# The two last sums of an output block: from VectorE reading PSUM to GpSimd reading a copy in SBUF

## The chip, the cores and the metric

The kernel runs on one core of a Trainium2 chip. The metric is the device time of one launch in microseconds (us). Three runs of the kernel before gave 1357.14, 1357.23 and 1366.95 us, so the median is 1357.23 us.

## The reference, cut to what matters

```python
def _moe2_ref(x, w_in, w_out):
    h = x @ w_in                 # (4608, 512) @ (512, 2048)
    g = h * np.cos(h)
    return (g @ w_out)           # (4608, 2048) @ (2048, 512)

def reference(**kwargs):
    attn_out = _attn_ref(q, k, v, g_norm)      # linear attention, RMS norm
    x = attn_out.transpose(0, 2, 1, 3).reshape(4608, 512)
    x = _moe_ref(x=x, ...)                     # 8 experts, the best one for each token
    return _moe2_ref(x=x, w_in, w_out)
```

Everything is float32. The change touches only the last function, and of it only the sums that make finished rows of the output.

## The kernel before, in words

The kernel has three stages. Attention and routing come first, then the experts, and from about 640 us to the end the last one, `_moe2_ref`, which this text calls the last stage. Each float32 product is done as three passes of TensorE (PE) over a high and a low part of both operands, so every result that feeds a product is split: ScalarE (ACT) writes the high part (`copy`, L1165-1166) and VectorE (DVE) subtracts it to get the low part (`sub`, L1171-1172).

In the last stage the 4608 tokens are cut into 9 blocks of 512 (`b`) and the 2048 hidden units into 8 slices of 256 (`q_`). One `step(i)` (L1258) handles one slice of one block, and there are 72 slices (`NS`). Both matrix products of a slice are done in Winograd's form, with 7 products of half-size blocks in place of 8. A step interleaves three things, all written out by hand in program order, and each engine works through its own instructions in that order:

- `h(...)`, the first product for slice `i`, into the PSUM banks `ha` (`xa`) and `hb` (`xb`), which DVE and ACT combine into the tiles `h` (`h1`, `h0`);
- for slice `i - 1` the rest of the cosine and the sums and splits that its second product needs;
- `o(...)`, the second product for slice `j = i - 2`, which adds into six PSUM banks, one for each of `a11`, `s2`, `a12`, `s3`, `a22` and `s1`. There is one bank of each name. In every step the `s1` product is the last one (L496).

The banks collect over the 8 slices of a block. With the block's last slice (`q_ == 7`, the flag `done`) and in the step after it (`q_ == 0` of the next block, the flag `after`) they are summed into output rows. `acc` holds a running sum of a seventh product, and two scratch tiles in SBUF, `E1` and `U2` (L1546), hold the partial sums: in the `done` step `E1` is the copy of `a11` (L1345), `U2 = E1 + s2` (L1356) and `acc = U2 + acc` (L1391); in the `after` step `E1 = U2 + s3` (L1318), the last reader of `U2`. What is left then is `late_sum` (L1218), called twice in the `after` step: it adds the bank `s1` to `E1` (call at L1358) and to `acc` (call at L1372), writes the right half of the 512 columns of the output tiles `o_sb1` and `o_sb0`, and issues for each tile two indirect DMAs (`out_row`, L1193) on GpSimd's (POOL's) queue, which put 128 rows each to their tokens' places. The profile calls `E1` "e", `U2` "u", the output tiles "o_sb" and the banks "o_s" and "o_a".

The first PE work of the next block that needs the bank `s1` is the `s1` product at the end of that same `after` step, so it waits until both sums have read the bank. There are 8 such boundaries between blocks. The end of the ninth block has its own function (`last_step`), with sums of its own.

Beside this, `pump()` (L1106) feeds in, step by step, the preparation of the next block's tokens (`tokens_of`, L368): DVE subtractions at L395 and L406, ACT copies at L401. Names for the lines that the prediction uses: `turns` (L1086, ACT), `parts` (L1089, DVE), `cosine` (L1092, ACT), the multiplications with the cosine at L1188 and L1325 (DVE), `add` (L1169, DVE). The weights stream in on SyncE's queue (`feed`, L513) and are not touched.

Of the kernel before, what the change touches and what calls it, by code (L numbers as in the profile page):

```python
# [14 lines left out]
ALU = mybir.AluOpType  # L15
# [21 lines left out]
def tile_kernel(ctx, tc, q, k, v, g_norm, emb, tau, w1, w2, w_in, w_out, out):  # L37
    nc = tc.nc
# [536 lines left out]
    if True:  # L575
        def pool(name, bufs, cx=actx, **kw):
            return cx.enter_context(tc.tile_pool(name=name, bufs=bufs, **kw))
# [60 lines left out]
        for i in range(2):  # L638
# [6 lines left out]
            out=ident, in_=ones, pattern=[[1, 128]], compare_op=ALU.is_equal, fill=0.0, base=0, channel_multiplier=-1  # L645
        )
        nc.gpsimd.affine_select(
            out=upper, in_=ones, pattern=[[1, 128]], compare_op=ALU.is_gt, fill=0.0, base=0, channel_multiplier=-1
# [11 lines left out]
        for i in range(2):  # L660
            nc.gpsimd.iota(
                out=nums[64 * i:64 * i + 64, :, 8], pattern=[[2 * S, 4]], base=i * S + 512, channel_multiplier=1
# [95 lines left out]
        def where(t):  # L758
            j, i = divmod(t, 9)
            return j, (2 * j + i // 4 if i < 8 else None), i % 4  # L760
# [224 lines left out]
        for t in range(NTILE):  # L985
            j, b, r = where(t)
# [60 lines left out]
    if True:  # L1047
# [55 lines left out]
        G, Y, bank = {}, {}, {}  # L1103
# [61 lines left out]
        def copy(out, in_):  # L1165
            nc.scalar.activation(out=out, in_=in_, func=ACTF.Copy)  # L1166

        def add(out, x, y):
            V.tensor_tensor(out=out, in0=x, in1=y, op=ALU.add)  # L1169

        def sub(out, x, y):  # L1171
            V.tensor_tensor(out=out, in0=x, in1=y, op=ALU.subtract)  # L1172

        def f32(x):
            return x.bitcast(F32)
# [17 lines left out]
        def out_row(b, t, th):  # L1193
            n = 4 * b + 2 * t + th
            ins = nc.gpsimd.indirect_dma_start(  # L1195
                out=out, out_offset=bass.IndirectOffsetOnAxis(ap=perm_i[:, n:n + 1], axis=0),
                in_=OUT[b][t][:, th], in_offset=None, bounds_check=NT - 1, oob_is_err=False,
            )
            tc.add_to_no_dep_group("rows", ins.ins)
            tc.declare_no_dep(ins.ins, group="rows", reason="every token has its own row")  # L1200

        def halves(x):
            return x.rearrange("p (t c) -> p t c", t=2)

        OUT = {}
# [3 lines left out]
        def bank_of(name, i):  # L1209
            if i == 0:  # L1210
                return any_bank("hps" if name == "ha" else "xp")[:, 0:256]
            elif (name, i) == ("ha", 2):
                p, name = ps_o, "o_s1"
            else:
                p = ps_h
            return p.tile([128, 512], F32, name=name, tag=name)[:, 0:256]

        def late_sum(b, t, x):  # L1218
            add(OUT[b][t][:, :, 256:512], halves(x), halves(bank[b, "s1"]))
            for th in range(2):  # L1220
                out_row(b, t, th)

# [35 lines left out]
        def step(i):  # L1258
# [4 lines left out]
            b, q_ = divmod(j, 8)  # L1263
            done = j >= 0 and q_ == 7
            after = j >= 8 and q_ == 0
# [11 lines left out]
            def o(kind="o"):  # L1277
                return out_product(pe(kind)) if j >= 0 else None
# [57 lines left out]
            if prev:  # L1336
                sub(s24[:, 1], r0[:, 1], s24[:, 0])
                copy(hi0, r0)
                copy(hi13, s13)
                copy(hi24, s24)  # L1340
                sub(lo0, r0, f32(hi0))
            if after:
                add(OUT[b - 1][1][:, :, 0:256], halves(E1), halves(bank[b - 1, "a22"]))
# [12 lines left out]
                add(U2, E1, bank[b, "s2"])  # L1356
            if after:
                late_sum(b - 1, 1, E1)  # L1358
            if new:
                xb = bank_of("hb", i)  # L1360
            h(xb, True)
# [6 lines left out]
            if done:  # L1368
                OUT[b] = [op.tile([128, 2, 512], F32, name=f"o_sb{t}", tag=f"o_sb{t}") for t in range(2)]
                add(OUT[b][0][:, :, 0:256], halves(E1), halves(bank[b, "a12"]))  # L1370
            if after:
                late_sum(b - 1, 0, Y["acc"])  # L1372
            if prev:
                sub(lo24, s24, f32(hi24))
            if new:
# [5 lines left out]
            if j >= 0 and q_ % 2:  # L1381
                t = o("t")
# [34 lines left out]
        for g in range(NC * 8 + LAG):  # L1417
# [21 lines left out]
            if g >= LAG:  # L1439
                c2, f2 = divmod(g - LAG, 8)  # L1440
                if g == 8 * NC - 1:
                    between = chain.from_iterable(layer2_parts(chunks[c2], x) for x in (5, 6, 7))
                    step(0)
                    store_y(chunks[c2])()
                elif g < 8 * NC:
                    layer2(chunks[c2], f2)
                if f2 == 7 and c2 < NC - 1:
                    flush = store_y(chunks[c2])
# [57 lines left out]
    if True:  # L1506
# [8 lines left out]
        op = pool("op", 1)  # L1515
# [30 lines left out]
        E1, U2 = (cc.tile([128, 512], F32, name=nm) for nm in ("e1", "u2"))  # L1546
        scr = lambda: sx.tile([128, 512], F32, name="sx", tag="sx")
        for i in range(1, NS + 2):
            b, q_ = divmod(i, 8)
            if i == (8 * b or 2) and b + 1 < NB:  # L1550
                coming[0] = tokens_of(b + 1, scr)
            step(i)
            for x in range(2 * i - 4, min(2 * i - 2, NB)):
                if x >= 0:
                    load_perm(x)
            if i == 8:
                permf.append(scr()[0:NTILE, 0:128])
                V.tensor_copy(out=permf[0], in_=perm_r)
            if i == 9:
                turn_perm()  # L1560
# [3 lines left out]
    if True:  # L1564
# [15 lines left out]
        with tc.For_i(0, n_more, 1):  # L1580
# [12 lines left out]
                out=osel, in0=osel, in1=oh.rearrange("p (o x) -> p o x", o=1).to_broadcast([128, 3, E]), op=ALU.mult  # L1593
# [54 lines left out]
            for m in range(NM):  # L1648
# [17 lines left out]
                for t, (i, n) in enumerate(TS):  # L1666
                    for x, (a, b_) in enumerate(PASS):
                        nc.tensor.matmul(
                            out=oc[t][0:n], lhsT=(hi, lo)[a][:, i:i + n], rhs=w[:, b_, 512:1024],
                            start=(m == 0 and x == 0), stop=(m == NM - 1 and x == 2),  # L1670
                        )
            for t, (i, n) in enumerate(TS):
# [3 lines left out]
                    out=out, out_offset=bass.IndirectOffsetOnAxis(ap=rows2[0:n, t:t + 1], axis=0),  # L1676
# [31 lines left out]
```

## Time and profile before

| | us |
|---|---|
| median of three runs | 1357.23 |
| the profiled execution's own time | 1357.04 |
| its span (first to last instruction) | 1355.5 |
| PE busy in the span | 1302.9 (96%) |
| DVE busy | 1102.2 (81%) |
| ACT busy | 846.2 (62%) |
| POOL busy | 175.4 (13%) |
| mean granted TensorE clock | 0.995 |

A row of a list of instructions in time order has the start in us, the duration in us, the engine, the line of the kernel, the operation, the tile written and the tiles read, and the count of instructions merged in the row; square brackets at the end hold the idle time of that engine just before, and what ended it. PE is the matmul, PEld the loading of its weights, which runs a little ahead of it. "POOL DMA_INDIRECT" is the time POOL takes to issue such a DMA. Consecutive DVE or ACT instructions overlap by some 0.1 us in these records.

### The profile page before, as it was taken

The numbers are of one execution on the slowest core, as the hardware profiler recorded it, in microseconds if no ns is written. First come the engines' busy times: TensorE is split into PE (matmuls) and PEld (weight loads), VectorE is DVE, ScalarE is ACT, GpSimd is POOL, SyncE is SP. The second block draws the span as 40 slices with busy tenths as digits, with TensorE's granted clock in tenths as the row PEclk, the third lists the DMA queues.
The fourth block names the chain that finished last, engine by engine and source line by source line (L and its number), as shares of the span: only waits on it lengthen the run. The fifth ranks groups of instructions, "written<-read, shape, count | busy, mean of one in ns | idle before, by whom it ended". The sixth has DMA issues, their size and how long they took to land.

```text
span 1355.5 us, 30321 instructions
## 1 busy us (share of the span) xinstructions
PE 1302.9 (96%) x10825; PEld 1279.5 (94%) x10825; DVE 1102.2 (81%) x2511; ACT 846.2 (62%) x1698; POOL 175.4 (13%) x286
## 2 busy tenths in 40 slices
PE   7998799999999999998999999999999999999997
PEld 6886799999999999998999999999999999999997
DVE  2567867788989888866889898888989889798876
ACT  4667454677666776545666666676666766666663
POOL 1234132113220000000001010000101001010101
PEclk9999999999999999999999999999999999999998
DMA  9999485788888798659998888888889889888884
GB/s 276 290 326 284 133 246 129 209 249 261 251 249 272 253 281 274 211 163 329 339 320 296 284 293 269 290 285 299 284 267 309 271 290 294 284 291 271 262 284 136
DMA packets 238102, 359.31 MB, mean 265 GB/s; under 512 B 26045, under 2 KB 114913, under 8 KB 236729
## 3 DMA queue, kind: packets, MB, share of 16 engines
q1 hardware_dynamic: 221480, 297.20, 69.3%
q0 software_dynamic: 16448, 60.08, 14.0%
q8 instruction: 89, 1.46, 0.4%
q14 instruction: 69, 0.56, 0.1%
q10 hardware_dynamic: 16, 0.02, 0.0%
HBM read 299.32 MB, written 57.89 MB: 264 GB/s over the span
## 4 chain that ended last, share of the span: by engine, by line
PE 66%; DVE 11%; issue 9%; DMA 5%; ACT 4%; SPq 3%; POOL 1%; POOLq 0%; ACTq 0%; DVEq 0%
PE ha L1124 12%; PE y L274 10%; PE hb L1124 9%; PE o_s L1137 9%; PE o_a L1137 9%; PE hps L253 7%; PE hb L1137 3%; PE xp L253 3%; DMA vr<-in_v 1%; DMA wa<-ws 1%; SPq L599 1%; DVE gx L180 1%; DVE ring L141 1%; DVE o_sb L1169 1%; ACT gx L174 1%
## 5 line engine op out<-in xcount | busy, mean ns | idle before, releaser
L274 PE MATMUL y<-h,ring 128*128 128x304 f32 x1536 | 235.8, 302 | 1.3 <-DVE yo L284 1.3
L274 PEld LDWEIGHTS y<-h,ring 128*128 128x128 f32 x1536 | 220.1, 188 | 1.7 <-ACT h L259 1.5
L253 PE MATMUL hps<-xT,ring 128*128 128x304 f32 x1152 | 182.8, 308 | 2.7 <-DVE xT L233 1.8
L253 PEld LDWEIGHTS hps<-xT,ring 128*128 128x128 f32 x1152 | 165.0, 190 | 4.1 <-DVE xT L233 2.2
L1092 ACT ACTIVATE u<-u,half_pi 128x512 f32<-128x512 f32 x142 | 102.3, 720 | 56.8 <-DVE u L1089 56.8
L1195 POOL DMA_INDIRECT out<-o_sb,perm_i x36 | 48.6, 1350 | 684.8 <-DVE o_sb L1169 576.5
L1086 ACT ACTIVATE u<-h 128x512 int32<-128x512 f32 x142 | 89.7, 632 | 71.0 <-DVE h L1169 65.0
L1089 DVE SCALAR_TENSOR_TENSOR u<-h,u 128x512 f32<-128x512 f32 x142 | 97.9, 689 | 24.8 <-ACT u L1086 22.9
L1137 PE MATMUL o_a<-ring,hi 128*128 128x256 f32 x568 | 107.9, 282 | 0.0
L141 DVE TENSOR_TENSOR ring<-raw,ring 128x1024 fp32r<-128x1024 f32 x72 | 87.8, 1219 | 21.3 <-ACT ring L140 20.6
L1166 ACT ACTIVATE hi<-u 128x512 fp32r<-128x512 f32 x142 | 88.6, 624 | 26.5 <-DVE u L1172 26.5
L1172 DVE TENSOR_TENSOR lo<-u,hi 128x512 fp32r<-128x512 f32 x142 | 96.9, 683 | 0.0
L259 ACT ACTIVATE h<-hps 128x304 fp32r<-128x304 f32 x96 | 40.3, 419 | 78.6 <-PE hps L253 74.5
L1137 PEld LDWEIGHTS o_a<-ring,hi 128*128 128x128 f32 x568 | 87.2, 189 | 0.0
L1166 ACT ACTIVATE hi<-h 128x256 fp32r<-128x256 f32 (+1 forms) x142 | 74.2, 522 | 19.6 <-PE o_a L1137 9.1
L1325 DVE TENSOR_TENSOR h<-h,u 128x512 f32<-128x512 f32 x71 | 49.0, 690 | 44.5 <-ACT u L1092 44.1
L1137 PE MATMUL o_a<-ring,lo 128*128 128x256 f32 x284 | 79.7, 281 | 0.0
L1172 DVE TENSOR_TENSOR lo<-h,hi 128x256 fp32r<-128x256 f32 (+1 forms) x142 | 78.2, 550 | 0.0
L140 ACT ACTIVATE ring<-raw 128x1024 fp32r<-128x1024 f32 x72 | 75.8, 1053 | 0.0
L1137 PE MATMUL o_s<-ring,hi 128*128 128x256 f32 x376 | 71.9, 283 | 0.0
L253 PE MATMUL xp<-xT,ring 128*128 128x304 f32 x384 | 60.1, 303 | 2.4 <-DVE xT L233 2.4
L260 DVE SCALAR_TENSOR_TENSOR h<-hps,h 128x304 fp32r<-128x304 f32 x96 | 44.4, 463 | 18.2 <-ACT h L259 16.3
(333 smaller groups left out, 3374.2 us busy)
## 6 DMA issues: line engine op xcount, KB each, us to landing
wb<-ws SPq DMA_DIRECT2D x224, 256.0 KB
wa<-ws SPq DMA_DIRECT2D x167, 256.0 KB
raw<-in_moe_w SPq DMA_DIRECT2D x144, 256.0 KB
ring<-ws SPq DMA_DIRECT2D x113, 256.0 KB
wb<-wo SPq DMA_DIRECT2D x96, 256.0 KB
ring<-wo SPq DMA_DIRECT2D x75, 256.0 KB
wa<-wo SPq DMA_DIRECT2D x73, 256.0 KB
wo<-wa SPq DMA_DIRECT2D x52, 256.0 KB
```

What stands on the lines that cost most here:

```text
L140: nc.scalar.activation(out=w[:, 0], in_=raw, func=ACTF.Copy)
L141: nc.vector.tensor_tensor(out=w[:, 1], in0=raw, in1=w[:, 0].bitcast(F32), op=ALU.subtract)
L253: nc.tensor.matmul(out=p[:, 0:CH], lhsT=w[:, a, k * 128:(k + 1) * 128], rhs=c["xT"][b_][k], start=(n == 0), stop=(n == 11),)
L274: nc.tensor.matmul(out=c["y"][d][:, 0:CH], lhsT=w[:, a, 512 + d * 128:512 + (d + 1) * 128], rhs=h[b_], start=(f == 0 and i == 0), stop=(f ...
L1086: nc.scalar.activation(out=n, in_=p, func=ACTF.Copy, scale=TURN, bias=0.25)
L1089: V.scalar_tensor_tensor(out=u, in0=p, scalar=TURN, in1=n, op0=ALU.mult, op1=ALU.subtract)
L1092: nc.scalar.activation(out=u, in_=u, func=ACTF.Sin, scale=2 * math.pi, bias=half_pi)
L1124: nc.tensor.matmul(out=out, lhsT=w[:, a, k * 128:(k + 1) * 128], rhs=x[xi][:, b_, k * 256:(k + 1) * 256], start=(start and n == 0), stop=( ...
L1137: nc.tensor.matmul(out=o[:, th * 256:th * 256 + 256], lhsT=G[j, name][a][:, th * 128:th * 128 + 128], rhs=w[:, b_, 0:256], start=(start an ...
L1166: nc.scalar.activation(out=out, in_=in_, func=ACTF.Copy)
L1172: V.tensor_tensor(out=out, in0=x, in1=y, op=ALU.subtract)
L1325: V.tensor_tensor(out=r0, in0=r0, in1=two_of(Y["u", 0]), op=ALU.mult)
```

## The change

In the `after` step, ACT copies the bank `s1` into `U2` (free since L1318 has read it). The two sums of `late_sum` are made by POOL, from `E1` or `acc` and from `U2`, all in SBUF. The second call of `late_sum` moves up to stand right behind the first. The DMAs of `out_row` stay on POOL's queue, in the same order among themselves.

```diff
         def late_sum(b, t, x):
-            add(OUT[b][t][:, :, 256:512], halves(x), halves(bank[b, "s1"]))
+            nc.gpsimd.tensor_tensor(out=OUT[b][t][:, :, 256:512], in0=halves(x), in1=halves(U2), op=ALU.add)
             for th in range(2):
                 out_row(b, t, th)
...
                 copy(hi24, s24)
+                if after:
+                    copy(U2, bank[b - 1, "s1"])
                 sub(lo0, r0, f32(hi0))
...
             if after:
                 late_sum(b - 1, 1, E1)
+                late_sum(b - 1, 0, Y["acc"])
...
-            if after:
-                late_sum(b - 1, 0, Y["acc"])
             if prev:
                 sub(lo24, s24, f32(hi24))
```

## Rows read from the trace of the kernel before

**Rows 1.** The page's first part: busy time of each engine in the span.
```profile
PE 1302.9 (96%) x10825; PEld 1279.5 (94%) x10825; DVE 1102.2 (81%) x2511; ACT 846.2 (62%) x1698; POOL 175.4 (13%) x286
```
**Rows 2.** Waits of PE's matmuls, 640 to 1350 us: total, times, longest.
```profile
PE o_s L1137 <- DVE o_sb L1169: 4.0, 8, 0.5
```
**Rows 3.** The chain that ended last: the same group in every second step.
```profile
786.16 1.44 PE hb L1137 x12
...
807.10 1.43 PE hb L1137 x12
...
827.12 1.44 PE hb L1137 x12
```
**Rows 4.** PE and PEld in time order at one boundary.
```profile
796.74 0.40 PE L1137 MATMUL o_a<-wb,hi 128*128 128x256 f32 x2
...
798.10 0.47 PE L1137 MATMUL o_s<-wa,hi 128*128 128x256 f32 x2 [0.49 <-DVE o_sb L1169]
...
801.03 0.78 PEld L1124 LDWEIGHTS ha<-ring,wa 128*128 128x128 f32 x6
...
806.13 0.76 PEld L1124 LDWEIGHTS ha<-ring,wb 128*128 128x128 f32 x6
```
**Rows 5.** DVE in time order at the same boundary.
```profile
794.81 0.68 DVE L1172 TENSOR_TENSOR lo<-u,hi 128x512 fp32r<-128x512 f32 x1
...
795.41 0.41 DVE L1169 TENSOR_TENSOR h<-five,ha 128x256 f32<-128x256 f32 x1
...
795.74 0.68 DVE L1169 TENSOR_TENSOR o_sb<-e,o_s 128x512 f32<-128x512 f32 x1
...
796.67 0.68 DVE L1089 SCALAR_TENSOR_TENSOR u<-h,u 128x512 f32<-128x512 f32 x1
...
797.27 0.68 DVE L1169 TENSOR_TENSOR o_sb<-acc,o_s 128x512 f32<-128x512 f32 x1
...
799.31 0.69 DVE L1089 SCALAR_TENSOR_TENSOR u<-h,u 128x512 f32<-128x512 f32 x1 [0.16 <-ACT u L1086]
...
800.59 0.68 DVE L395 TENSOR_TENSOR sx<-xb,sx 128x512 f32<-128x512 f32 x1
...
805.66 0.41 DVE L1169 TENSOR_TENSOR h<-five,ha 128x256 f32<-128x256 f32 x1
...
806.83 0.69 DVE L1089 SCALAR_TENSOR_TENSOR u<-h,u 128x512 f32<-128x512 f32 x1 [0.43 <-ACT u L1086]
```
**Rows 6.** ACT in time order at the same boundary.
```profile
793.78 0.63 ACT L1166 ACTIVATE hi<-u 128x512 fp32r<-128x512 f32 x1 [0.37 <-DVE u L1172]
...
795.91 0.63 ACT L1086 ACTIVATE u<-h 128x512 int32<-128x512 f32 x1 [1.50 <-DVE h L1169]
...
800.62 0.36 ACT L1166 ACTIVATE one<-ha 128x256 f32<-128x256 f32 x1
```
**Rows 7.** ACT's copies of a whole bank, 740 to 1270 us: busy us, mean ns.
```profile
L1166 ACT ACTIVATE e<-o_a 128x512 f32<-128x512 f32 x7 | 4.1, 581 | 0.0
```
**Rows 8.** POOL in time order at the same boundary.
```profile
796.70 1.51 POOL L1195 DMA_INDIRECT out<-o_sb,perm_i  x1 [74.30 <-DVE o_sb L1169]
...
800.32 1.21 POOL L1195 DMA_INDIRECT out<-o_sb,perm_i  x1 [0.30 <-DVE u L1089]
```
**Rows 9.** POOL's groups by shape, whole span: busy us, mean ns, idle before.
```profile
L878 POOL TENSOR_TENSOR exc<-exc,ohc 128x8 f32<-128x8 f32 x16 | 3.3, 209 | 6.9 <-DVE ohc L873 6.3
...
L675 POOL MEMSET kvb<- 128x576 f32 x3 | 1.6, 572 | 0.0
L865 POOL TENSOR_TENSOR w<-w,tie 128x24 f32<-128x24 f32 x8 | 2.0, 254 | 32.7 <-DVE w L864 32.6
...
L643 POOL MEMSET ones<- 128x128 f32 x1 | 0.3, 271 | 0.0
```
**Rows 10.** DVE and POOL in time order near 117 us, in the first stage.
```profile
117.20 1.21 DVE L141 TENSOR_TENSOR ring<-raw,ring 128x1024 fp32r<-128x1024 f32 x1
...
117.28 1.20 POOL L879 TENSOR_TENSOR run<-exc,ohc 128x8 f32<-128x8 f32 x1
```

## The prediction, as put on record before the run

> **What bounds the kernel now.** I read the page's busy shares first, then the chain of waits that ended last, then PE's own waits in the last stage, and at last one boundary between two blocks on all engines in order of time. PE is busy 96% of the span [rows 1], so a change is worth what it takes off PE's waits, or what it adds to them. The chain runs through PE in almost every piece of the last stage. The reader is to look at one group that comes back in every second step: from 807.10 to 827.12 it takes 20.02 us, two steps with PE at its pace, and from 786.16 to 807.10 it takes 20.94 us [rows 3]. That longer pair holds a boundary, and the excess is 0.92 us. There are 8 boundaries [rows 2], so all that any change to the boundary can win is about 8 x 0.92 = 7.4 us, half a per cent.
>
> Where does the 0.92 us go? The list in time order shows three places. First, the six matmuls into `a22` begin at 796.74 and take 0.72 us as any six do (half of the 1.44 of twelve), so the `s1` product could start at 797.46; it starts at 798.10, released by the second late sum on DVE [rows 3, 4]. That is 0.64 us. Second, at 801.03 the weights of an `ha` product are loaded some 0.1 us late, behind ACT's copy `one`, which ends at 800.62 + 0.36 = 800.98 [rows 4, 6]. Third, at 806.13 the same happens behind DVE's sum `h<-five,ha`, which ends at 805.66 + 0.41 = 806.07 [rows 4, 5]. The last two matter more than their size: ACT and DVE are late there too, so a PE that arrives earlier merely waits longer. DVE has no idle time between 799.31 and the 0.43 us ahead of 806.83 [rows 5].
>
> **The change part by part.** *The copy on ACT.* It follows the copy `hi24`, which runs from 793.78 to 794.41; a copy of a whole bank takes 0.58 us, so `U2` is ready about 794.9 [rows 6, 7]. ACT's next instruction starts at 795.91 after 1.50 us of idling for a DVE sum, so the copy lies inside that idle time and costs nothing; if the cover were gone it would cost 0.58 us of ACT's time. The bank is then free 2.5 us before 797.46, and PE's wait of 0.64 us goes away in full.
>
> *The two sums leave DVE.* They sit at 795.74 and 797.27 [rows 5], and DVE starts a following instruction some 0.6 us after the one before, so 1.2 us of DVE's time is set free. But not all of it comes out as earlier work. The next long DVE instruction, `parts` at 796.67, needs ACT's `turns`, which runs from 795.91 to 796.54 [rows 5, 6] and starts behind `h<-five,ha`, which does not move. So `parts` can start at 796.57, 0.10 us earlier. The second sum stood between `parts` and the low part of `s24`; without it that low part ends about 0.7 us earlier, and ACT's next `turns`, which overwrites what it reads, follows. By then the cosine and its multiplication are the later chain, and I get `parts` of the next half at about 798.9 in place of 799.31. So DVE and ACT gain about 0.42 us of the 0.64 that PE gains, and at 801.03 and 806.13 PE waits for them. With nothing else, the boundary gains 0.42 us.
>
> *The two sums on POOL.* The trace shows no POOL addition of this size. From below: a fill grows from 271 ns at 128 columns to 572 ns at 576, 0.67 ns a column [rows 9]; an addition has two inputs, and two such passes over 512 columns plus 0.2 us are 0.9 us. From above: POOL's additions take 209 ns at 8 columns and 254 ns at 24 [rows 9], 2.8 ns a column, which at 512 gives 254 + 488 x 2.8 = 1.6 us. I take 1.3 us, between the two; the addition rows are the same operation but a long way off, so both ends stay in the range. That POOL itself is busy longer costs nothing: it idles 74 us before each boundary [rows 8], the output tiles are not reused for most of a block, and `acc` is not overwritten before the next step.
> [...]
>
> *What the POOL sums do to DVE.* This decides the sign. Near 117 us a POOL addition of 8 columns, which takes 0.21 us elsewhere, takes 1.20 us [rows 9, 10]. It starts 0.08 us after a DVE subtraction with both inputs in SBUF and ends 0.07 us after that one. So a POOL instruction that reads SBUF stands still while DVE reads two SBUF tensors, and it got its turn as soon as that one DVE instruction was over. I read this as something that one of the two engines holds at a time, and conclude that a POOL sum will hold up a DVE instruction with two SBUF inputs in the same way, for the sum's whole duration. The trace before cannot show that side, since POOL's additions there are tiny; so its price goes from nothing to the whole 1.6 us, and I take the whole of the 1.3 us.
> [...]
>
> Now the schedule. The first POOL sum is ready about 795.05. DVE is then in a low-part subtraction (both inputs in SBUF) until 794.81 + 0.68 = 795.49 [rows 5], so the sum runs from 795.49 to 796.79. DVE's next two sums read PSUM and go on; `parts`, both inputs in SBUF, waits from 796.57 to 796.79. That costs 0.22 us, and the gain of 0.42 shrinks to 0.20. POOL then issues the two DMAs of the first tile; first to third such DMA is 800.32 - 796.70 = 3.6 us before [rows 8], so with the first starting 0.3 us behind the sum the second sum is ready at about 800.7. DVE is there in its stretch without idle time, in the preparation of tokens, with two SBUF inputs each; the instruction of 800.59, now at 800.39, ends at 801.07. The second sum takes over for 1.3 us, and the next DVE instruction starts at 802.37 where it would have started at 800.99: 1.38 us lost. Net on DVE: 1.38 - 0.20 = 1.18 us later than before. `h<-five,ha` then ends at 807.25 in place of 806.07, and PE, which waits for it at 806.13, is 1.18 us later than before. The `ha` product's neighbour `hb` waits for the same DVE stretch a little earlier, for less. PE has no idle time later to win that back.
>
> Sum: 8 x 1.18 = 9.4 us. The profiled execution took 1357.04 us, which stands 0.2 us below the median; 1357.0 + 9.4 = 1366.4 us, 0.7% slower. With a POOL sum of 0.9 us the first sum costs nothing and the boundary loses 0.98 - 0.42 = 0.56 us, in all 4.5 us (1361.5). With 1.6 us it loses 1.68 - 0.42 + 0.52 = 1.78 us, in all 14.2 us (1371.2).
>
> **The rivals.** *POOL does not hold DVE up.* If only POOL waits, or if the two share at a finer grain than an instruction, the gain of 0.42 us a boundary is left: 8 x 0.42 = 3.4 us, 1353.6 us. For it: no DVE row shows a delay beside POOL. Against it: those POOL instructions are too short to show one, and the 1.20 us row shows a whole instruction's exclusion. If ACT and DVE should keep up with PE after all, the ceiling of 7.4 us gives 1349.6.
> *POOL's sum is far slower than its rows say.* If it takes 2.5 us, DVE loses 2.58 - 0.42 + (2.5 - 1.08) = 3.6 us at a boundary, in all 29 us, 1386 us. It decides above 1.5 us, where the slowdown passes 1%. For it: 2.8 ns a column is read off two tiny shapes. Against it: nothing in the rows is slower than that.
> *The hold-up falls where DVE has time.* If the second sum comes to lie behind 806, where DVE idles 0.43 us and more, gain and loss cancel: about 1357 us. Against it: POOL's queue puts it at 800.7, six us too early.
>
> **How the numbers follow.** The hold-up as worked out: 0.57. No hold-up: 0.31. Cancelling: 0.05. Much slower sums: 0.07. The likeliest case has its own range of 1361.5 to 1371.2; the range that takes in the case without hold-up goes from 1352 to 1371. About 1% (13.6 us) is what a measurement of this kernel can tell from no change. Faster by more than that is beyond the ceiling of 7.4 us: 0.01. Slower by more needs sums of nearly 1.6 us or the slow case: 0.12. The rest, 0.87, is within 1%.
>
> **What would show it right or wrong.** PE's wait for `o_sb` at the `s1` product must be gone, and the copy of the bank must start about 794.3 into ACT's idle time. Two POOL additions of about 1.3 us must stand at each boundary, the first running to about 796.8, the second about 801 to 802.4. DVE must show a gap or a stretched instruction with two SBUF inputs beside the second of about its length. PE must show 8 new waits of over 1 us for `h<-five,ha` or `h<-two,hb`, and a pair of steps with a boundary must last about 22.1 us in place of 20.94. If the DVE instructions beside POOL's sums keep their usual spacing, the hold-up is wrong and the pair lasts about 20.5 us.

## The result, and the profile after

The changed kernel took 1369.44 us (median of 13 runs), beside 1361.33 us for the kernel before (also 13 runs, the first three among them): a ratio of 1.0079, 95% interval 1.0062 to 1.0097, so it is 0.8% slower. The profiled execution took 1365.98 us, against 1357.04 before. The forecast was 9.4 us or 0.7% slower, by POOL's sums holding up DVE.

PE's new waits come first. These are the waits of PE's weight loads in the last stage of the kernel after (what waited, on what; us in total, times, longest; PEld is the loading of PE's weights):

```profile
PEld hb L1124 <- DVE h L1169: 10.6, 7, 1.5
PEld ha L1124 <- DVE h L1169: 3.1, 8, 0.4
PEld ha L1124 <- ACT h L1166: 2.0, 8, 0.3
```

The wait for `o_sb` of [rows 2] is gone, and a wait for DVE's sums `h` has come, 1.5 us long at 7 of the 8 boundaries. At the boundary that the rows of before show (all of this trace runs 0.73 us earlier there), this is POOL in time order:

```profile
794.26 1.66 POOL L1219 TENSOR_TENSOR o_sb<-e,u 128x512 f32<-128x512 f32 x1 [73.81 <-ACT u L1166]
796.19 1.22 POOL L1195 DMA_INDIRECT out<-o_sb,perm_i  x1 [0.28 <-POOL o_sb L1219]
797.72 1.16 POOL L1195 DMA_INDIRECT out<-o_sb,perm_i  x1 [0.30 <-issue]
798.90 1.30 POOL L1219 TENSOR_TENSOR o_sb<-acc,u 128x512 f32<-128x512 f32 x1
```

DVE in time order, to be held against [rows 5]:

```profile
794.07 0.68 DVE L1172 TENSOR_TENSOR lo<-u,hi 128x512 fp32r<-128x512 f32 x1
794.68 0.41 DVE L1169 TENSOR_TENSOR h<-five,ha 128x256 f32<-128x256 f32 x1
795.01 0.41 DVE L1169 TENSOR_TENSOR h<-one,hb 128x256 f32<-128x256 f32 x1
795.85 0.69 DVE L1089 SCALAR_TENSOR_TENSOR u<-h,u 128x512 f32<-128x512 f32 x1 [0.43 <-ACT u L1086]
...
798.27 2.49 DVE L1089 SCALAR_TENSOR_TENSOR u<-h,u 128x512 f32<-128x512 f32 x1 [0.24 <-ACT u L1086]
...
804.57 0.41 DVE L1169 TENSOR_TENSOR h<-two,hb 128x256 f32<-128x256 f32 x1
...
806.44 0.41 DVE L1169 TENSOR_TENSOR h<-five,ha 128x256 f32<-128x256 f32 x1
```

The row to look at is the one at 798.27: the same instruction on the same shapes, 2.49 us in place of 0.69, and it ends 0.56 us after the second POOL sum (798.90 + 1.30 = 800.20). Beside the first POOL sum nothing is stretched (0.41, 0.41 and 0.69 us). Everything behind on DVE is late, and PE, in time order, waits for it:

```profile
785.27 0.40 PE L1137 MATMUL hb<-ring,hi 128*128 128x256 f32 x2
...
805.04 0.97 PE L1124 MATMUL hb<-ring,ring 128*128 128x256 f32 x6 [1.30 <-DVE h L1169]
...
806.91 0.97 PE L1124 MATMUL ha<-ring,wb 128*128 128x256 f32 x6 [0.18 <-DVE h L1169]
807.73 0.40 PE L1137 MATMUL hb<-wa,hi 128*128 128x256 f32 x2
```

The first and the last of these rows begin the group of [rows 3]: 807.73 - 785.27 = 22.46 us for the pair of steps with a boundary, where it was 20.94. On the way PE waits 1.30 us at an `hb` product, for DVE's sum `h<-two,hb`, and then 0.18 us at the `ha` product, for `h<-five,ha`. ACT did what was foreseen: the copy of the bank at 793.59 lies in idle time, of which 1.01 us is still left behind it.

```profile
793.59 0.58 ACT L1166 ACTIVATE u<-o_s 128x512 f32<-128x512 f32 x1
795.18 0.64 ACT L1086 ACTIVATE u<-h 128x512 int32<-128x512 f32 x1 [1.01 <-DVE h L1169]
```

Over all 8 boundaries the pairs took 178.4 us in place of 168.0, which is 10.4 us: 1.2 to 1.5 us at each of the first seven, 0.1 at the last. The two profiled spans differ by 8.9 us only, and the rest lies in other places: this execution reached the last stage 2.0 us sooner, and lost 0.6 us once ahead of a boundary. So the length of a boundary pair is the sharper measure, and it is used beside the ratios from here on. It repeats within 0.03 us over most boundaries of a trace (22.44 to 22.47 us at six of the eight here), while the medians of the kernel before, taken beside the runs below, lie between 1358.63 and 1361.33 us.

### The profile page after: what moved, and what is told of

It reads as the page before. It is cut to its first block, busy times and chain, and to the rows that moved or that the text cites. A ratio compares the mean times of both kernels' runs of the same rounds, so it can differ in the third digit from the quotient of the medians.

```text
span 1364.4 us, 30365 instructions
## 1 busy us (share of the span) xinstructions
PE 1308.6 (96%) x10825; PEld 1282.8 (94%) x10825; DVE 1109.0 (81%) x2495; ACT 849.8 (62%) x1706; POOL 190.6 (14%) x302
## 5 line engine op out<-in xcount | busy, mean ns | idle before, releaser
L1089 DVE SCALAR_TENSOR_TENSOR u<-h,u 128x512 f32<-128x512 f32 x142 | 112.5, 792 | 29.1 <-ACT u L1086 26.8
L1219 POOL TENSOR_TENSOR o_sb<-e,u 128x512 f32<-128x512 f32 x8 | 13.3, 1658 | 613.8 <-ACT u L1166 613.8
L1124 PE MATMUL ha<-ring,wb 128*128 128x256 f32 x390 | 57.9, 284 | 1.7 <-DVE h L1169 1.1
```

Source lines behind the costliest of these rows:

```text
L1089: V.scalar_tensor_tensor(out=u, in0=p, scalar=TURN, in1=n, op0=ALU.mult, op1=ALU.subtract)
L1124: nc.tensor.matmul(out=out, lhsT=w[:, a, k * 128:(k + 1) * 128], rhs=x[xi][:, b_, k * 256:(k + 1) * 256], start=(start and n == 0), stop=( ...
```

## The experiments

The theory is that a POOL instruction that reads SBUF keeps DVE from starting or finishing one with two SBUF inputs. Its rivals: the cost is in the copy or in the new order; each POOL sum costs its own length wherever it lies; any POOL work does it. "Pair" is that of the boundary shown above.

| kernel | pair, us | sum of the 8 pairs | ratio to before (95%) |
|---|---|---|---|
| before | 20.94 | 168.0 | |
| after | 22.46 | 178.4 | 1.0079 (1.0062 to 1.0097) |
| `a_copy_dve` | 20.95 | 167.5 | 0.9995 (0.9983 to 1.0007) |
| `b_first_pool` | 20.88 | 166.9 | 0.9988 (0.9974 to 1.0001) |
| `c_second_pool` | 22.30 | 177.3 | 1.0073 (1.0047 to 1.0100) |
| `d_sums_first` | 21.38 | 170.4 | 1.0028 (1.0009 to 1.0048) |
| `e_fill` | 20.63 | 165.1 | no ratio (one run) |
| `f_one_input` | 21.48 | 171.0 | no ratio (one run) |
| `g_late` | 20.63 | 165.1 | 0.9978 (0.9965 to 0.9992) |
| `h_a22_later` | 20.18 | 161.7 | 0.9953 (0.9935 to 0.9972) |
| `i_no_pool` | 20.12 | 161.3 | 0.9961 (0.9947 to 0.9975) |
| `j_a22_alone` | 20.94 | 168.0 | 1.0005 (0.9990 to 1.0020) |

**Both sums back on DVE, the copy kept** (`a_copy_dve`; edits are against the kernel after):

```diff
-            nc.gpsimd.tensor_tensor(out=OUT[b][t][:, :, 256:512], ...)
+            V.tensor_tensor(out=OUT[b][t][:, :, 256:512], ...)
...
-                late_sum(b - 1, 0, Y["acc"])      # back in its old place, behind parts_of
```

> Theory (a POOL sum that reads SBUF holds up DVE instructions with two SBUF inputs): with both sums back on DVE, reading the copy U2, no DVE instruction is stretched. PE's 0.64 us wait at the s1 product is gone, but DVE carries as much as before, so PE waits for ACT's copy and DVE's sum instead: a pair of steps with a boundary takes 20.8 to 20.95 us (20.94 before, 22.46 after the change), ratio 0.999 to 1.000. Rival (the copy into U2 on ACT, or the lost slot on ACT, costs the time): the pair stays near 22.4 us, ratio 1.007.

Measured: 20.95 us, no change from before. The copy costs nothing, and it wins nothing by itself. These are the waits of PE's weight loads in this kernel:

```profile
PEld ha L1124 <- ACT one L1166: 2.8, 7, 0.4
PEld ha L1124 <- ACT h L1166: 2.7, 8, 0.4
```

The 0.64 us saved at the `s1` product is waited for a little later, for two copies by ACT.

**One sum on POOL** (`b_first_pool`: the first; `c_second_pool`: the second; the other one on DVE, reading `U2`; in `b_first_pool` the second call of `late_sum` is also back in its old place):

```diff
-            nc.gpsimd.tensor_tensor(...)
+            (nc.gpsimd if t else V).tensor_tensor(...)      # b; c has (V if t else nc.gpsimd)
```

> Only the first sum on POOL, the second on DVE from U2 in its old place. Theory: the first sum falls where DVE reads PSUM or waits for ACT, so it holds up nothing that counts; POOL's addition shows some 1.6 us, no DVE instruction is stretched by over 0.2 us, the pair takes 20.8 to 20.9 us, ratio 0.998 to 1.000. Rival (each POOL sum costs DVE its own length wherever it falls): the pair takes some 21.7 us, ratio 1.004.

> Only the second sum on POOL, the first on DVE from U2. Theory: this sum alone makes the loss; one DVE instruction is stretched by 1.2 to 1.9 us, the pair takes 22.0 to 22.6 us, ratio 1.006 to 1.010. Rival (each POOL sum costs the same): some 21.7 us, ratio 1.004.

Measured: 20.88 and 22.30 us. The two sums are the same instruction on the same shapes; the first is free, and the second alone makes 22.30 - 20.94 = 1.36 of the 1.52 us. That excludes a fixed price for a POOL sum. In `c_second_pool` another DVE instruction is hit, a sum of 256 columns that takes 0.41 us elsewhere. DVE and then POOL in time order:

```profile
804.38 1.94 DVE L1169 TENSOR_TENSOR u<-h 128x256 f32<-128x256 f32 x1
```

```profile
804.71 1.31 POOL L1219 TENSOR_TENSOR o_sb<-acc,u 128x512 f32<-128x512 f32 x1
```

It ends 0.30 us after the sum, as the one of 512 columns ended 0.56 us after: most of the instruction's usual 0.41 or 0.69 us is still to be done when the sum ends.

**Both sums first, then the four DMA issues** (`d_sums_first`):

```diff
             nc.gpsimd.tensor_tensor(out=OUT[b][t][:, :, 256:512], ...)
-            for th in range(2):
-                out_row(b, t, th)
...
                 late_sum(b - 1, 0, Y["acc"])
+                for t in (1, 0):
+                    for th in range(2):
+                        out_row(b - 1, t, th)
```

> Both sums on POOL, right behind each other, then the four DMA issues. Theory that the hold begins while POOL still issues the DMA ahead of the second sum (so that DVE loses 1.80 us to a sum of 1.30): with no DMA ahead of it DVE loses at most 1.3 us, its instruction (now the first parts of the step, near 795.9) shows at most 2.0 us in place of 2.49, and the pair takes 21.8 to 22.1 us, ratio 1.004 to 1.006. Rival (the hold is the second sum's own, and longer than its record): the stretch stays at 1.8 us and the pair near 22.4 us, ratio 1.007.

Measured: 21.38 us, less than either theory gave. POOL and then DVE in time order:

```profile
795.61 1.66 POOL L1219 TENSOR_TENSOR o_sb<-e,u 128x512 f32<-128x512 f32 x1 [72.03 <-ACT u L1166]
797.22 1.82 POOL L1219 TENSOR_TENSOR o_sb<-acc,u 128x512 f32<-128x512 f32 x1
```

```profile
797.20 0.69 DVE L1089 SCALAR_TENSOR_TENSOR u<-h,u 128x512 f32<-128x512 f32 x1 [0.43 <-ACT u L1086]
797.81 1.78 DVE L1172 TENSOR_TENSOR lo<-u,hi 128x512 fp32r<-128x512 f32 x1
```

Here one can see both directions in four rows. DVE's `parts` came 0.02 us ahead of the second sum and ran its usual 0.69; the sum waited for it and took 1.82 us. DVE's next instruction then waited for the sum: 1.78 - 0.69 = 1.09 us lost, where it was 2.49 - 0.69 = 1.80 with two DMA issues ahead of the sum. The pair grows by less, 21.38 - 20.63 (`e_fill`, below, where nothing holds DVE) = 0.75 us, because DVE has idle time right behind: the 0.19 us that it idles ahead of L1188 in the kernel after are gone, and 0.16 of the 0.24 us ahead of the next `parts` are left. The sum also lies beside other instructions than before, so this run does not separate the DMA issue from the place.

**What of a POOL instruction holds DVE** (`e_fill`, `f_one_input`; the second sum alone is replaced, so the bank `s1` is missing from that quarter of the output, and in `e_fill` `acc` too):

```diff
+            if t:
                 nc.gpsimd.tensor_tensor(...)
+            else:
+                for _ in range(2):                                     # e_fill
+                    nc.gpsimd.memset(OUT[b][t][:, :, 256:512], 0.0)
...
+                nc.gpsimd.tensor_copy(out=OUT[b][t][:, :, 256:512], in_=halves(x))   # f_one_input
```

> As after the change, but in place of the second sum POOL only fills the same half of the tile, twice (the second sum is left out; POOL is busy about as long, some 1.1 us, and reads no SBUF tensor). Theory (POOL's reading of SBUF is what holds DVE): the instruction parts behind it takes its usual 0.69 us and the pair with a boundary takes 20.5 to 20.8 us in place of 22.46. Rival (any POOL instruction of that length holds DVE, or it is POOL's writing): parts is stretched by 1 us or more and the pair stays at 22 us or above.

> As after the change, but the second sum is a POOL copy of acc, one input in place of two (the bank's part of these columns is left out). Theory: one SBUF input is enough to hold DVE, for the copy's own length of 0.5 to 0.9 us and what it begins under the DMA issue ahead of it (0.5 us in the kernel after the change); parts takes 1.5 to 2.1 us, the pair 21.4 to 22.0 us. [...]

Measured: 20.63 and 21.48 us. POOL, then DVE, in `e_fill`:

```profile
800.83 1.16 POOL L1195 DMA_INDIRECT out<-o_sb,perm_i  x1 [0.30 <-issue]
801.99 1.13 POOL L1223 MEMSET o_sb<- 128x512 f32 x2
```

```profile
801.38 0.69 DVE L1089 SCALAR_TENSOR_TENSOR u<-h,u 128x512 f32<-128x512 f32 x1 [0.24 <-ACT u L1086]
801.99 0.42 DVE L1169 TENSOR_TENSOR u<-h 128x256 f32<-128x256 f32 x1
802.32 0.42 DVE L1172 TENSOR_TENSOR lo<-h,hi 128x256 fp32r<-128x256 f32 x1
```

And in `f_one_input`:

```profile
801.59 0.98 POOL L1222 COPY o_sb<-acc 128x512 f32<-128x512 f32 x1
```

```profile
800.97 1.12 DVE L1089 SCALAR_TENSOR_TENSOR u<-h,u 128x512 f32<-128x512 f32 x1 [0.24 <-ACT u L1086]
802.02 0.83 DVE L1169 TENSOR_TENSOR u<-h 128x256 f32<-128x256 f32 x1
```

1.1 us of POOL writing costs DVE nothing, and neither does the DMA issue ahead of it, in whose record `parts` starts: it takes its usual 0.69 us. A POOL copy with one SBUF input costs DVE 0.43 + 0.42 = 0.85 us, spread over two instructions, and the pair is longer by just that (21.48 - 20.63). So it is POOL's reading, and one input is enough. I had expected all of it in `parts` (1.5 to 2.1 us, measured 1.12), and a copy of 0.5 to 0.9 us, which was my estimate with no row behind it; the copy took 0.98.

**The second sum on DVE one step later** (`g_late`; the first stays on POOL):

```diff
             if new:
                 add(h0[:, 0:256], one, xb)
+            if j >= 8 and q_ == 1:
+                late_sum(b - 1, 0, Y["acc"])      # on DVE, from U2
+            if new:
                 parts_of(i, 1)
```

> First sum on POOL (which held up nothing), second on DVE from U2, one step later, ahead of parts, where DVE idles some 0.4 us. Theory: PE's wait at the s1 product is gone and DVE is free of both sums in its full stretch; left are PE's waits for the copy of h0 (0.3 us) and for the copy one (0.1 to 0.2 us): the pair takes 20.5 to 20.8 us, ratio 0.997 to 0.999. Rival (DVE's work at the boundary is conserved and PE waits for it anyway): 20.9 us, ratio 1.000.

Measured: 20.63 us, 0.9978. The early copy and a DVE free of both sums in its full stretch do win something: 0.31 us at a boundary. In the list of PE's waits one is left there, for ACT's copy into `h0` (8 times, up to 0.3 us).

**And DVE's sum with `a22` later** (`h_a22_later`, on top of `g_late`): the addition of L1343 goes behind `turns_of(i, 1)`, so that DVE makes the sum with `five`, for which `turns` waits, before it.

```diff
-            if after:
-                add(OUT[b - 1][1][:, :, 0:256], halves(E1), halves(bank[b - 1, "a22"]))
...
                 add(h1[:, 256:512], five, xa)
                 turns_of(i, 1)
+            if after:
+                add(OUT[b - 1][1][:, :, 0:256], halves(E1), halves(bank[b - 1, "a22"]))
```

> As the run before, and DVE's sum with the bank a22 moved behind the one with five, so that ACT's turns starts 0.6 us earlier. Theory (ACT's and DVE's chain through turns is what PE waits for after the s1 product): PE's waits for ACT's copies of h0 and ha shrink by most of their 0.45 us, the pair takes 20.1 to 20.5 us, ratio 0.995 to 0.998. Rival (these waits come from another place): no change from the run before.

Measured: 20.18 us where two undisturbed steps take 20.02, and a ratio of 0.9953: faster than both kernels. In this kernel POOL's sum starts 0.10 us after DVE's subtraction has ended (796.00 + 0.68 = 796.68) and takes 1.29 us, which is its own length. DVE's sum with `a22`, which has one input in PSUM, lies inside it and is not stretched:

```profile
796.78 1.29 POOL L1219 TENSOR_TENSOR o_sb<-e,u 128x512 f32<-128x512 f32 x1 [65.61 <-ACT u L1166]
```

```profile
796.93 0.68 DVE L1169 TENSOR_TENSOR o_sb<-e,o_a 128x512 f32<-128x512 f32 x1
```

**Which part of that wins** (`i_no_pool`: as `h_a22_later`, but both sums on DVE one step later; `j_a22_alone`: the kernel before with the `a22` sum moved and nothing else):

```diff
+            if j >= 8 and q_ == 1:                     # i_no_pool
+                late_sum(b - 1, 1, E1)                 # both on DVE
+                late_sum(b - 1, 0, Y["acc"])
```

> As the fastest run so far (a22 later), but without any POOL sum: both sums on DVE from U2, one step later. Theory (the gain comes from the order on DVE and the early copy of the bank, POOL's share is one sum of 0.6 us of DVE time): DVE has 0.43 us of idle time ahead of parts there for 1.2 us of sums, so parts comes some 0.8 us late in that step and PE may wait some 0.3 us for ACT's copies; the pairs with and behind a boundary together are 0.2 to 0.6 us over 40.05, ratio 0.9955 to 0.9985. Rival (the gain needs POOL to carry the first sum): 0.9 us over, ratio 1.000.

> The kernel before with nothing but DVE's sum with the bank a22 moved behind the one with five: no copy of s1, both late sums on DVE from PSUM in their old places. Theory (PE waits for a chain on DVE and ACT that this sum delays by 0.6 us): parts and with it the second late sum come some 0.5 us earlier, so PE's wait at the s1 product shrinks from 0.64 us to 0.1 or 0.2, and the pair takes 20.2 to 20.5 us, ratio 0.996 to 0.998. Rival (the wait for the bank can only go with the copy): the pair stays over 20.8 us, ratio 0.999 to 1.000.

Measured: `i_no_pool` 0.9961, its pair 20.12 and the next 20.46 (20.32 at most boundaries), together 0.5 us over 40.05, the length of two undisturbed pairs (0.4 at most boundaries); `h_a22_later` has 20.18 and 20.01, together 0.1 over (0.2 at most boundaries). So POOL's first sum is worth some 0.2 us at most boundaries, and the order on DVE, the later place of the sums and the early copy together win the rest; by time the two kernels can't be told apart. For `j_a22_alone` my expectation was wrong: nothing moved, and the wait that was to shrink stands there as ever:

```profile
PEld o_s L1137 <- PE o_a L1137: 5.4, 8, 0.7
```

I had not followed it through: DVE is without idle time up to the second late sum, so moving one instruction inside that stretch leaves its end where it was. In `h_a22_later` the same move won 20.63 - 20.18 = 0.45 us; there the bank was copied early and both late sums had left the stretch. No run has the move with the copy alone, so which of the two it needs is not shown.

## Why the prediction was right or wrong

**The bound and the ceiling** hold: 7.4 us was said to be all there is to win at the boundaries, and `h_a22_later` has won 168.0 - 161.7 = 6.3 of it.

**The copy on ACT** was right: it starts where it was said (793.59 + 0.73 = 794.32, said 794.3) and costs nothing, and PE's wait at the `s1` product is gone.

**DVE's gain of 0.42 us without a hold-up** was mis-sized: the kernels without one (`e_fill`, `g_late`) gain 20.94 - 20.63 = 0.31. DVE's second `parts`, put at about 798.9, came at 798.27 + 0.73 = 799.00 in the clock of before, 0.31 us ahead of 799.31 and not 0.42. The list of places where PE waits also lacked one: the `ha` product right behind the `s1` product, which now waits up to 0.3 us for ACT's copy into `h0`.

**POOL's sum of 1.3 us** was right, though it was only taken as a value between 0.9 and 1.6, and that it fits so well is partly luck: 1.30 us for the second, and the first's 1.66 holds 0.36 us of waiting for a DVE subtraction that had started 0.19 us before.

**The hold-up of DVE**, argued from one row about POOL waiting for DVE, was right in its direction and its kind; the exchange of one sum at a time, the fill and the copy show it. In these runs DVE lost 0 us to the fills, which only write, and 0.85 to 1.80 us to the POOL instructions that read SBUF while it had two SBUF inputs to read.

**The price of each sum** is the step that failed: the mechanism was right, and the term of the second sum was too small. For the first I said 0.22 us; it is nothing, because `parts` starts 0.07 us before the record of that sum ends (795.85 against 794.26 + 1.66 = 795.92) and is not stretched. For the second I said 1.38 us at about 800.7; it costs 1.80 us and comes 1.1 us sooner (798.90 + 0.73 = 799.63), because the two DMA issues ahead of it took 1.22 and 1.16 us, where I had used the 3.6 us from first to third of before. So it meets `parts` and not the preparation of tokens, and takes 0.50 us more than its own 1.30 (last section). Net, a boundary loses 1.80 - 0.31 = 1.49 us by these terms, 1.52 by the rows, where 1.18 was forecast.

**Where PE waits for it** was wrong in its order: I had PE wait at the `ha` product, and at `hb` for less; it waits 1.30 us at `hb` and then 0.18 us at `ha`, and at 7 boundaries where I said 8.

**Eight equal boundaries** was wrong too: the last one loses 0.10 us. In the code it is the one boundary without preparation of a next block's tokens, whose three subtractions take DVE some 1.8 us at the others (801.36 to 803.19), about as much as the hold-up costs. DVE is held there as well:

```profile
1293.67 2.49 DVE L1089 SCALAR_TENSOR_TENSOR u<-h,u 128x512 f32<-128x512 f32 x1 [0.24 <-ACT u L1086]
```

Over all 142 instructions the group of `parts` grew from 97.9 to 112.5 us, 14.6 us, or 1.8 for each of 8 sums. That the totals come close, 10.4 us in the boundaries against 9.4, and 1365.98 us in the profiled execution against 1366.4, is luck: seven boundaries lose more than forecast and one far less, and this execution reached the last stage 2.0 us sooner.

**The chances**: no hold-up had 0.31 and much slower sums 0.07, and both are excluded by rows. A change within 1% was given 0.87, and 0.8% it is. But the step that 1% is what a measurement of this kernel can tell from no change failed: it was set down without a row behind it, and with 13 runs of each kernel the interval reaches from 0.6 to 1.0%, clear of no change.

## What to carry to other kernels

An idle POOL is not free help for a busy DVE: in these runs a POOL sum or copy that reads SBUF cost DVE 0.85 to 1.80 us where it met DVE instructions with two SBUF inputs, not far from its own length (0.98 us the copy, 1.30 the sum). Here such a POOL instruction cost nothing where DVE read PSUM or waited for ACT (beside the first sum its instructions took 0.42 us in `b_first_pool`, elsewhere 0.41, and 0.68 us in `h_a22_later`); try such a place, and look in the profile for a DVE row that is longer than its siblings of the same shape. Before moving instructions off a full engine, look for a later place on the same engine: here the kernel with both sums on DVE, one step later where DVE idles (`i_no_pool`), was as fast as the best one with a sum on POOL.

## What the runs showed of the hardware that was not expected

The hold seems to begin before the POOL sum's record does. In the kernel after, DVE's `parts` starts at 798.27, 0.63 us before the second sum and inside the record of the DMA issue ahead of it, and has 0.56 of its 0.69 us left when the sum ends: 1.80 us lost to a sum of 1.30. In `c_second_pool` the held instruction starts 0.33 us before the sum's record and loses 1.94 - 0.41 = 1.53 us. It is not the DMA issue that holds DVE, for in `e_fill` `parts` starts inside the same issue and is not stretched. With no DMA issue ahead of the sum (`d_sums_first`) 1.09 us are lost. In `f_one_input` the POOL copy behind a DMA issue holds two DVE instructions by 0.43 and 0.42 us and lets the first finish in between. No run here shows why the hold begins there; the rows would look like this if POOL's record began later than its reading, which is not shown either.
